# A recurrence and a dense block on one core: the first weights in 512 columns, own terms of two more units on TensorE, another written order

## The chip, the core and the metric

The kernel runs on one core of a Trainium2 chip. Five engines work side by side: TensorE (PE, with its weight loads shown apart as PEld), VectorE (DVE), ScalarE (ACT), GpSimd (POOL) and SyncE (SP). SP, ACT and POOL also issue transfers between HBM and the on-chip memory. The metric is the device time of one execution in microseconds, as a median over runs.

## The reference

Two blocks follow each other. The first is a recurrence with one state per head; its output, reshaped to 3072 rows of 384, goes through a dense block with 2048 hidden columns.

```python
# r, k, v: (4 batches, 8 heads, 768 steps, 48); w, u: (8, 48)
for t in range(S):
    kt, vt, rt = (k[:, :, t], v[:, :, t], r[:, :, t])
    cur = np.einsum('bhd,bhe->bhde', u[None] * kt, vt)
    y[:, :, t] = np.einsum('bhd,bhde->bhe', rt, state + cur)
    state = w[None, :, :, None] * state + np.einsum('bhd,bhe->bhde', kt, vt)
...
x = np.ascontiguousarray(attn_out.transpose(0, 2, 1, 3)).reshape(B * S, H * D)
h = x @ w_in          # (3072, 384) @ (384, 2048)
g = h - np.tanh(h)
return (g @ w_out).astype(np.float32)
```

The term with `u` is the *own term*: a step's own k and v, weighted by u. The weights `w_in` and `w_out` arrive as 64-bit floats, everything else as 32-bit.

## The kernel before, in words

**Units.** The recurrence is cut into 24 units, numbered 0 to 23: 64 steps of two batches with all heads, 12 chunks of time by two pairs of batches. A unit loads r, k and v (two halves of 96 KB each), turns r and k on TensorE, scales them by powers of the decay (`rT` and `kT`), and multiplies the two within the chunk (`levels`, rows `rT,kT` of L606). A predicated copy puts the part under the diagonal into the tile `at`. Then come the products with v (`outputs`, rows `at,vt`), with the state (`rT,state`) and for the next state (`vt,kw`). ACT copies the result into `xt`, the input of the dense block. Two units make one dense block of 256 rows; there are 12.

**Own terms.** Two ways exist. A unit with `n < OWN` makes `kU` from kT by four ACT operations (L709), multiplies it with rT on TensorE (rows `rT,kU`) and puts the diagonal into `at` by a predicated copy on DVE (L821). Any other unit multiplies r, k and u on DVE (`rk`, L696 and L824), sums over the head (`du`, L700) and writes the eight diagonals with eight ACT operations (L704). Before, `OWN` is 1, so unit zero alone goes the first way.

**The dense block.** A tile is 256 hidden columns of one block: six products for `h` (L217), five ACT and three DVE operations that make `g` from it, and four products for the output (`o`, L254; later a form with seven products, L307). The first pass goes over six blocks and the first four of the sixteen column groups of 128, and the units 0 to 11 run beside it.

**Weights.** They are loaded in 16 pieces of 128 x 768 numbers of 64 bits (768 KB): of each four, the first two are w_in (256 columns each), the others w_out. A w_in piece comes as four DMAs, two of 288 KB by SP and two of 96 KB by POOL, into one of four staging buffers; then DVE and ACT convert it to 32 bits in seven steps (L185 to L191, five on DVE).

**The order.** Nothing is scheduled while the program runs: the string `ORDER` names the tasks one after the other, two characters each, and each engine executes its own in that order. A task that waits holds up everything behind it on its engine. Names past the last task are *fills*, products of the identity with itself without use for the result (L534). The DMAs of SP and ACT together use eight landing marks in turn (`DMAHW0` to `DMAHW7` below), so that a ninth is issued only when the first has landed.

## Time and profile before

| | us |
|---|---|
| median of 3 runs | 582.31 (581.24 to 583.12) |
| the profiled execution | 582.57 |
| its span | 580.8 |
| PE busy | 562.5 (97%) |
| DVE busy | 429.9 (74%) |
| ACT busy | 404.3 (70%) |
| POOL busy | 199.9 (34%) |

The span goes from the first instruction to the last; the profiled execution's own time is 1.8 us longer. A share of busy time is a mean over stages: ACT's 70% is made of stages near 100% and stages near 55%. In groups of instructions each row has line, engine, operation, output and inputs, shapes and count, then busy time and mean ns, then the engine's idle time ahead of them and what ended it. In a timeline the row begins with start and length in us; neighbours on one engine are pipelined and overlap a little, so that the distance of two starts is the pace.

### The profile page before, as it was taken

What the parts mean: (1) busy time and instruction counts of PE and PEld (TensorE: products, weight loads), DVE (VectorE), ACT (ScalarE), POOL (GpSimd) and SP (SyncE); (2) the same over time, 40 slices, a digit from 0 to 9 for tenths busy, and PEclk for the clock granted to TensorE, in tenths of its full rate; (3) what the DMA queues carried; (4) which work ended last, traced back from release to release, by engine and by line L of the source; (5) the groups of instructions that cost most, each with busy time, mean ns of one, the idle gap of its engine ahead of it and who ended that gap; (6) DMA issues with size and microseconds to landing.
All of it is one profiled execution on the core that took longest, in us unless ns stands there. A gap on an engine that the chain in (4) does not pass through costs nothing.

```text
span 580.8 us, 14137 instructions
## 1 busy us (share of the span) xinstructions
PE 562.5 (97%) x5487; PEld 480.4 (83%) x5487; DVE 429.9 (74%) x720; ACT 404.3 (70%) x926; POOL 199.9 (34%) x366
## 2 busy tenths in 40 slices
PE   7699999999999999999999999999999999999995
PEld 4467777777776789999888889989999988999994
DVE  4899878999998787967699796567676766454534
ACT  2699999999977566545884787577577568765550
POOL 5201111300000233546256184273455253463430
PEclk9999999999999999999999999999999999999999
DMA  8987857594620000132344451441233000010001
GB/s 137 171 199 145 140 117 118 120 173 109 142 64 5 1 1 1 28 56 44 54 67 85 61 105 23 68 89 17 45 63 61 2 21 16 5 30 2 19 11 32
DMA packets 138549, 38.48 MB, mean 66 GB/s; under 512 B 130761, under 2 KB 132905, under 8 KB 138473
## 3 DMA queue, kind: packets, MB, share of 16 engines
q1 hardware_dynamic: 130140, 29.71, 28.7%
q0 software_dynamic: 4992, 6.99, 5.3%
q10 hardware_dynamic: 3340, 0.79, 0.9%
q8 instruction: 45, 0.74, 0.5%
q14 instruction: 32, 0.25, 0.2%
HBM read 31.66 MB, written 4.72 MB: 63 GB/s over the span
## 4 chain that ended last, share of the span: by engine, by line
PE 87%; DMA 4%; ACT 3%; DVE 2%; issue 1%; SPq 1%; POOL 0%; ACTq 0%; DVEq 0%; POOLq 0%
PE h L217 41%; PE p L307 26%; PE o L254 10%; PE yk_ps L606 6%; DMA rt<-in_r_dram 2%; PE x_ps L656 1%; DMA vt<-in_v_dram 1%; DMA xt<-rest 1%; ACT at L704 1%; PE x_ps L606 1%; SPq L644 1%; ACT xt L765 0%; PE p L254 0%; PE x_ps L534 0%; POOL xt L786 0%
## 5 line engine op out<-in xcount | busy, mean ns | idle before, releaser
L217 PE MATMUL h<-xt,w_in_sb 128*128 128x256 f32 x1152 | 267.3, 381 | 0.2 <-DMA xt<-rest 0.2
L217 PEld LDWEIGHTS h<-xt,w_in_sb 128*128 128x128 f32 x1152 | 214.9, 190 | 32.5 <-DVE g L242 1.5
L290 POOL TENSOR_TENSOR sg<-g 128x256 f32<-128x256 f32 x69 | 55.1, 800 | 197.7 <-DVE g L246 130.1
L242 DVE TENSOR_TENSOR g<-h,th 128x512 f32<-128x512 f32 x96 | 65.8, 686 | 67.9 <-ACT tg L233 25.2
L229 ACT ACTIVATE s<-h 128x512 f32<-128x512 f32 x96 | 57.1, 594 | 54.3 <-PE h L217 47.2
L307 PE MATMUL p<-mixed,sg 128*128 128x192 f32 x426 | 92.3, 327 | 0.0
L244 DVE TENSOR_TENSOR tg<-s,tg 128x512 f32<-128x512 f32 x96 | 69.3, 724 | 29.2 <-ACT s L224 19.4
L233 ACT ACTIVATE tg<-h 128x512 f32<-128x512 f32 x96 | 56.9, 594 | 41.9 <-PE h L217 29.9
L246 DVE COPY_PREDICATED g<-small,tg 128x512 f32<-128x512 int32 x96 | 72.0, 761 | 12.0 <-ACT small L235 9.0
L231 ACT ACTIVATE th<-h 128x512 f32<-128x512 f32 x96 | 56.7, 593 | 32.7 <-PE h L217 32.6
L307 PEld LDWEIGHTS p<-mixed,sg 128*128 128x128 f32 x426 | 73.3, 190 | 1.3 <-issue 0.3
L307 PE MATMUL p<-w_out_sb,g 128*128 128x192 f32 x284 | 70.4, 330 | 0.3 <-DVE o L335 0.3
L235 ACT ACTIVATE small<-s,smallb 128x512 f32<-128x512 f32 x96 | 68.5, 721 | 1.2
L254 PE MATMUL o<-w_out_sb,g 128*128 128x384 f32 x192 | 67.3, 489 | 0.0
L786 POOL DMA_DIRECT2D xt<-rest x66 | 32.5, 496 | 91.7 <-ACT rest L765 91.1
L224 ACT ACTIVATE s<-s 128x512 f32<-128x512 f32 x96 | 60.7, 633 | 1.4
L307 PEld LDWEIGHTS p<-w_out_sb,g 128*128 128x128 f32 x284 | 50.6, 190 | 3.1 <-DVE o L335 0.6
L254 PEld LDWEIGHTS o<-w_out_sb,g 128*128 128x128 f32 x192 | 35.8, 190 | 19.4 <-DVE parts L267 0.2
L704 ACT ACTIVATE at<-same,du 128x64 f32<-128x64 f32 x184 | 48.2, 342 | 0.5 <-DVE du L700 0.4
L292 POOL TENSOR_TENSOR sg<-sg,g 128x128 f32<-128x128 f32 x69 | 39.1, 569 | 3.1
L294 POOL TENSOR_TENSOR sg<-sg,g 128x128 f32<-128x128 f32 x69 | 37.2, 542 | 3.4
L307 PE MATMUL p<-mixed,g 128*128 128x192 f32 x142 | 34.7, 326 | 0.0
(127 smaller groups left out, 654.1 us busy)
## 6 DMA issues: line engine op xcount, KB each, us to landing
st<-in_moe_w_out_dram SPq DMA_DIRECT2D x8, 768.0 KB, 5.5
st<-in_moe_w_in_dram SPq DMA_DIRECT2D x16, 288.0 KB, 5.9
rt<-in_r_dram SPq DMA_DIRECT2D x46, 96.0 KB, 3.6
vt<-in_v_dram SPq DMA_DIRECT2D x46, 96.0 KB, 3.7
kt<-in_k_dram SPq DMA_DIRECT2D x44, 96.0 KB, 3.2
out_dram<-o POOLq DMA_DIRECT2D x44, 96.0 KB, 2.2
st<-in_moe_w_in_dram POOLq DMA_DIRECT2D x16, 96.0 KB, 5.9
parts<-in_k_dram SPq DMA_DIRECT2D x48, 32.0 KB, 2.1
```

The source lines that it names most:

```text
L217: self.nc.tensor.matmul(t.h2[:, z], self.w_in_sb[:, t.f // 2, kk, z * 128 : (z + 1) * 128], self.xts[t.j][:, kk].rearrange("p b t -> p (b ...
L224: A.activation(t.s, t.s, AF.Square, scale=G3)
L229: A.activation(out, t.h, AF.Arctan, scale=G2)
L231: A.activation(out, t.h, AF.Tanh)
L233: A.activation(out, t.h, AF.Tanh, scale=G1)
L235: A.activation(out, t.s, AF.Relu, bias=self.smallb, scale=-1.0)
L242: V.tensor_tensor(t.g, t.h, t.th, ALU.subtract)
L244: V.tensor_tensor(t.tg, t.s, t.tg, ALU.mult)
L246: V.copy_predicated(t.g, t.small.bitcast(I32), t.tg)
L254: self.nc.tensor.matmul(self.outs[i], t.g2[:, z, i * C : (i + 1) * C], self.w_out_sb[:, t.f + z, :], start=t.first and z == 0, stop=t.last ...
L290: add(t.s4[:, :2], g[:, 0::3], g[:, 1:2].to_broadcast([128, 2, C]), ALU.add)
L307: self.nc.tensor.matmul(ps[bank][:, half * n : (half + 1) * n], a, b, start=t.first and half == 0, stop=t.last, skip_group_check=True)
```

## The change

`OWN` becomes 3: units one and two take the way of unit zero. A pair of w_in pieces is loaded at once, 512 columns of a row in one run, into one staging buffer of double size (`si`, one of them), from which each half is converted by itself; w_out keeps its size with two buffers (`so`). Of the first pair all four DMAs are issued by SP, later ones two by SP and two by POOL as before. `ORDER` is another string from the first line to the last; its rows tell a reader nothing, so one of each is shown.

```diff
--- before.py
+++ after.py
@@ -32,7 +32,7 @@
 L = 2
 FIRST = 6
 PASSES = 4, 4, 8
-OWN = 1
+OWN = 3
 SWAP = 2
 ALONE = 2
 LATE = 4
@@ -43,50 +43,49 @@
 
 DIGITS = "0123456789ABCDEFGHIJKLMNOPQRSTUVWXYZabcdefghijklmnopqrstuvwxyz+_"
 ORDER = (
-    "00010J2f2g2h2i2j2k2l2m2n0HbWbX02030K040605bWbWbW2o2q3534363231332r2t0I2s07370A0FbWbX080B0C2u2x2y38392v092w3U0D3C"
...
+    "00012V2Q2P2R2T2S2U2W2X0H0KbCbD02030I040J0605bD2Y2a2r2q2s2o2b072c0AbD080B0C2e2n2p2h092f2i0D2g2Z2d2t2u2v0LbCbD2j0M"
...
 )
 
 
@@ -152,21 +151,34 @@
         if n % 4 > 1:
             f = slice(2 * of, 2 * of + 2)
             return self.w_out_sb[:, f, :], [(slice(0, 128), w_out.rearrange("(ko ki) f -> ki ko f", ki=128)[:, f, :])]
-        cols = w_in[:, of * 256 : (of + 1) * 256]
-        parts = []
+        return self.w_in_sb[:, of], self.spread(w_in[:, of * 256 : (of + 1) * 256])
+
+    def spread(self, cols):
+
+        d, parts = self.d, []
         for i in range(2):
             main = cols[: d.NK * 2 * d.D].rearrange("(k r) f -> r k f", k=d.NK)[i * d.D : (i + 1) * d.D]
             rest = cols[(2 * d.NK + i) * d.D :][: d.D].rearrange("(k x) f -> x k f", k=d.NK)
             parts += [(d.HEAD[i], main), (slice(i * PAD + d.D, (i + 1) * PAD), rest)]
-        return self.w_in_sb[:, of], parts
+        return parts
+
+    def wide(self, n):
+
+        return n % 4 < 2 and self.sources[0].dtype == I64
 
     def load(self, n, i, queue):
 
-        dst, parts = self.piece(n)
-        if self.sources[n % 4 > 1].dtype == I64:
+        if self.wide(n):
             if n not in self.staged:
-                self.staged[n] = self.stage.tile([128, self.COLS], I64, name="st", tag="st", bufs=4)
-            dst = self.staged[n].rearrange("p (k f) -> p k f", k=dst.shape[1])
+                self.staged[n] = self.staged[n + 1] = self.stage.tile([128, 2 * self.COLS], I64, name="si", tag="si", bufs=1)
+            dst = self.staged[n].rearrange("p (k f) -> p k f", k=self.d.NK)
+            parts = self.spread(self.sources[0][:, n // 4 * 512 : (n // 4 + 1) * 512])
+        else:
+            dst, parts = self.piece(n)
+            if self.sources[n % 4 > 1].dtype == I64:
+                if n not in self.staged:
+                    self.staged[n] = self.stage.tile([128, self.COLS], I64, name="so", tag="so", bufs=2)
+                dst = self.staged[n].rearrange("p (k f) -> p k f", k=dst.shape[1])
         to, src = parts[i]
         queue.dma_start(out=dst[to], in_=src)
 
@@ -175,12 +187,13 @@
 
 
         V, A = self.nc.vector, self.nc.scalar
-        dst = self.piece(n)[0].rearrange("p k f -> p (k f)")
-        st = self.staged.pop(n)
-        words = st.bitcast(U32).rearrange("p (n t) -> p n t", t=2)
-        lo, hi = words[:, :, 0], words[:, :, 1]
-        lo_f = st.bitcast(F32).rearrange("p (n t) -> p n t", t=2)[:, :, 0]
-        power = self.stage.tile([128, self.COLS], U32, name="power", tag="power", bufs=2)
+        dst, st = self.piece(n)[0], self.staged.pop(n).rearrange("p (k f) -> p k f", k=self.piece(n)[0].shape[1])
+        if self.wide(n):
+            st = st[:, :, n % 2 * 256 : (n % 2 + 1) * 256]
+        words = st.bitcast(U32).rearrange("p k (f t) -> p k f t", t=2)
+        lo, hi = words[..., 0], words[..., 1]
+        lo_f = st.bitcast(F32).rearrange("p k (f t) -> p k f t", t=2)[..., 0]
+        power = self.stage.tile([128, self.COLS], U32, name="power", tag="power", bufs=2).rearrange("p (k f) -> p k f", k=dst.shape[1])
         bits = dst.bitcast(U32)
         yield V.tensor_scalar(power, hi, 0x7FF00000, None, ALU.bitwise_and)
         yield V.tensor_scalar(bits, hi, 0xFFFFF, 0x100000, ALU.bitwise_and, ALU.bitwise_or)
@@ -586,9 +599,11 @@
         loads, converted = [], []
         for n in range(weights.count):
 
-            queues, data = (("SP",), (3.0,)) if n % 4 > 1 else (("SP", "POOL") * 2, (1.2, .95) * 2)
-            of = [add(e, .55, lambda n=n, i=i, e=e: weights.load(n, i, e_of[e]), [converted[n - 4] if n >= 4 else None],
-                      data=x, gated=True) for i, (e, x) in enumerate(zip(queues, data))]
+            wide, freed = weights.wide(n), [converted[n - 4]] if n >= 4 else []
+            queues, data = (("SP",), (3.0,)) if n % 4 > 1 else (("SP", "SP" if n < 2 else "POOL") * 2, (1.3, .98) * 2 if wide else (1.2, .95) * 2)
+            if not wide or n % 4 == 0:
+                of = [add(e, .55, lambda n=n, i=i, e=e: weights.load(n, i, e_of[e]), freed + ([converted[n - 3]] if wide and freed else []),
+                          data=x, gated=True) for i, (e, x) in enumerate(zip(queues, data))]
             if weights.sources[n % 4 > 1].dtype != I64:
                 converted.append(of[-1])
                 continue
```

What the string does is seen in each engine's own list. SP at the start, before (names: `st` staging, `rt`, `first_k`, `vt` the loads of unit zero, with numbers that are one higher for unit one):

```order
L171 DMA st<-in_moe_w_in_dram 48x3x256
L644 DMA rt_106<-in_r_dram 64x8x48
L644 DMA first_k_122<-in_k_dram 64x8x48
L644 DMA vt_116<-in_v_dram 64x8x48 [waits DMAHW0_49]
L171 DMA st<-in_moe_w_in_dram 48x3x256 [waits DMAHW1_49]
L644 DMA first_k_123<-in_k_dram 64x8x48 [waits DMAHW4_49]
L644 DMA rt_107<-in_r_dram 64x8x48 [waits DMAHW5_49]
```

and now:

```order
L659 DMA vt_116<-in_v_dram 64x8x48
L659 DMA rt_106<-in_r_dram 64x8x48
L659 DMA first_k_122<-in_k_dram 64x8x48
L183 DMA si<-in_moe_w_in_dram 48x3x512 [waits DMAHW0_49]
L183 DMA si<-in_moe_w_in_dram 16x3x512 [waits DMAHW3_49]
L183 DMA si<-in_moe_w_in_dram 16x3x512 [waits DMAHW4_49]
L183 DMA si<-in_moe_w_in_dram 48x3x512 [waits DMAHW6_49]
L659 DMA first_k_123<-in_k_dram 64x8x48 [waits DMAHW7_49]
L659 DMA rt_107<-in_r_dram 64x8x48 [waits DMAHW0_49]
```

Unit zero's loads moved ahead of all weights; the weights of two pieces stand as one group between unit zero and unit one, and what POOL issued of the first piece is in it.

DVE from unit zero's own-term copy into `at_132` on, before:

```order
L821 COPY_PREDICATED at_132<-same,x_ps_146 128x512
L807 TENSOR_TENSOR kw_113<-first_k_123,w_down 128x8x48
L807 TENSOR_TENSOR kw_112<-first_k_122,w_down 128x8x48
L696 TENSOR_TENSOR rk<-rt_107,first_k_123 128x384
L185 TENSOR_SCALAR power<-st 128x768
L186 TENSOR_SCALAR w_in_sb<-st 128x768
L660 TENSOR_TENSOR rT<-x_ps_150,power 128x512
L824 TENSOR_TENSOR rk<-rk,ub 128x384
L700 TENSOR_REDUCE du<-rk 128x8
L665 TENSOR_TENSOR kT<-x_ps_150,inverse 128x512
L189 SCALAR_TENSOR_TENSOR w_in_sb<-w_in_sb,st 128x768
L807 TENSOR_TENSOR kw_112<-kt,w_down 128x8x48
```

(L190 and the copy into `at_133`, L830, follow), and now:

```order
L836 COPY_PREDICATED at_132<-same,x_ps_146 128x512
L822 TENSOR_TENSOR kw_112<-first_k_122,w_down 128x8x48
L198 TENSOR_SCALAR power<-si 128x768
L199 TENSOR_SCALAR w_in_sb<-si 128x768
L198 TENSOR_SCALAR power<-si 128x768
L822 TENSOR_TENSOR kw_113<-first_k_123,w_down 128x8x48
L199 TENSOR_SCALAR w_in_sb<-si 128x768
L675 TENSOR_TENSOR rT<-x_ps_150,power 128x512
L680 TENSOR_TENSOR kT<-x_ps_150,inverse 128x512
L202 SCALAR_TENSOR_TENSOR w_in_sb<-w_in_sb,si 128x768
L845 COPY_PREDICATED at_133<-before,x_ps_150 128x512
L203 SCALAR_TENSOR_TENSOR power<-si,power 128x768
```

Behind these stand unit one's own-term copy (L836 into `at_133`) and then, ahead of unit two's copies, one `kw`, four long conversion steps (L204, L202, L203, L204), unit two's scaling of r, two short steps of the w_out piece and the flag. The first conversion steps of both halves moved ahead of unit one's scalings, and the three operations of its own terms (`rk`, `rk`, `du`) are gone.

ACT from unit one's `xt` (a row of 128x2x3x64) on, before:

```order
L765 COPY xt<-yk_ps 128x2x3x64
L795 ACTIVATE state_127<-yk_ps,power 128x2x48 x4
L704 ACTIVATE at_132<-same,du 128x64 x4
L572 ACT_TABLE_LOAD
L572 ACTIVATE warm<-one 128x1
L704 ACTIVATE at_132<-same,du 128x64 x4
L187 ACTIVATE power<-power,p_bias 128x768
L188 ACTIVATE st<-st 128x768
L229 ACTIVATE s<-h 128x512
```

and now:

```order
L780 COPY xt<-yk_ps 128x2x3x64
L707 COPY kT<-x_ps_146 128x512
L810 ACTIVATE state_127<-yk_ps,power 128x2x48 x4
L724 ACTIVATE kU<-kT,w_u 128x128 x4
L200 ACTIVATE power<-power,p_bias 128x768
L201 ACTIVATE so<-so 128x768
L246 ACTIVATE tg<-h 128x512
L242 ACT_TABLE_LOAD
L242 ACTIVATE s<-h 128x512
```

Unit two's own terms are four operations without the table load between them; the load moved behind the first `tg`.

More of the change, by code (lines that the diff above doesn't have):

```diff
@@ new lines @@
+    "3C0S2y2k2x3D3E0N2w0T3A2l2z0O2+393B2_0PbD33303F0Z342mbD310Q0U323I3X3J0V3b350R3a3c3K360W0F3M373L7v380X3Y3Z3N3G3H0a"
+    "3Q0E0b440Y0c3O45467w3R0d0s3P423h7z3g41430e3S7x3d7+3l0f3i3T853e3f3m3j4V3U863n4S3k4F3V3o4U4W4G3q0g4R4T3p0h4H7y483r"
+    "7_47494BbE3s4I814+804_504A3t3W4C824D3u834f4E3_3v89404b4y4K4J4g3+4x4z3x4h87843z4L883y3w4i5O0q0i4c8C4X8A4M4Y4Z4j8D"
+    "5M4a554N8J4d594O5L5N0j8K5P5Q4e4P8B0p5A4k4Q0k5B8E0l8V5s4l8M5r5t0m8L545u5C565v5w0n4m8N5Z8O8W0o4n528Q51538F58574o5a"
+    "8G6J5b8P4t4p6I6K8H4v8R5E4r6F8I8S5D4s6GbG6H4w4q8T5c4u5F5S635d5G5R5T645V8X0r5U655H5W8U6m5X5I5y5Y8j5J8Z5x5z8a6l6n5e"
@@ L90 @@
+    "ZfaCZ1Z3aEZ4Z2a0Z5Z6a1ZRZ7ZsZ8ZBZ9aHaQZDa3ZAaeZta4aSaFZSaGaIaRaJZgaTa5aUaVZha6aXa7aWafaKaYZCa+ahaLaiaMagZvalZuaj"
+    "a_Zwb0b3a8aZb2amb1a9akb4anaNaaabb5aOb6aoacb7apaqadaratauasavawb8axayazb9bAbB"
 )
```

78 lines of the change are left out of this document (35 added, 43 removed).

## The prediction

> **What bounds the kernel now.** I read the stage table first, in stretches of 10 us and, where data is short, of 5.
>
> ```profile
> 0.00:10.00 10.00, 7.96 (x23) 3.98 (x23) 4.71 (x13) 1.62 (x2) 5.76 (x26) 1.00 0.81 140
> 10.00:20.00 10.00, 7.76 (x198) 5.60 (x196) 7.35 (x14) 5.76 (x17) 3.97 (x12) 1.00 0.99 152
> 20.00:30.00 10.00, 5.52 (x142) 4.03 (x143) 6.97 (x12) 6.87 (x23) 1.01 (x2) 1.00 1.15 179
> 30.00:40.00 10.00, 10.00 (x243) 7.29 (x238) 9.28 (x17) 9.51 (x26) 0.00 (x0) 1.00 0.85 173
> 40.00:60.00 20.00, 19.17 (x347) 15.06 (x338) 19.82 (x35) 19.67 (x61) 3.92 (x8) 1.00 0.80 163
> ...
> 5.00:10.00 5.00, 4.49 (x18) 2.33 (x16) 3.55 (x5) 1.62 (x2) 1.48 (x3) 1.00 1.25 200
> 10.00:15.00 5.00, 3.84 (x88) 2.87 (x90) 2.38 (x5) 1.99 (x7) 2.01 (x8) 1.00 0.86 131
> ...
> 40.00:45.00 5.00, 4.48 (x103) 3.76 (x94) 5.00 (x9) 4.88 (x17) 2.31 (x5) 1.00 0.99 252
> ```
>
> The busy columns are PE, PEld, DVE, ACT, POOL; the last three are granted clock, DMA share and GB/s. PE stands idle 2.04 + 2.24 + 4.48 = 8.8 us before 30 us and hardly afterwards, so only the first stage has time to give. From 30 to 60 us DVE and ACT are nearly full as well. Some of the busy PE time yields nothing: products of the identity that fill waits (L534), here beside the one own-term product.
>
> ```profile
> L534 PE MATMUL h<-ident 128*128 128x512 f32 x12 | 7.1, 701 | 1.5 <-POOL ident masks.py:199 1.5
> L534 PE MATMUL h<-ident 128*128 128x256 f32 x8 | 2.9, 456 | 0.0
> L534 PE MATMUL x_ps<-ident 128*128 128x512 f32 x6 | 2.7, 592 | 0.0
> L534 PE MATMUL x_ps<-ident 128*128 128x256 f32 x4 | 1.3, 405 | 0.0
> L606 PE MATMUL x_ps<-rT,kU 48*64 48x64 f32 x32 | 1.0, 236 | 1.0 <-ACT kU L709 1.0
> ```
>
> These fills sum to 14.0 us. With the 8.8 idle, 22.8 of the first 40 us or so bring the result no nearer. Why PE waits there is in the chain of waits (start, length, what):
>
> ```profile
> 4.19 6.26 DMA vt<-in_v_dram
> ...
> 15.20 7.33 DMA rt<-in_r_dram
> ...
> 27.56 2.21 issue
> ```
>
> Loads set the first 23 us; the 2.21 us belong to ACT, which loads a table before it finishes unit two's own terms. The units' steps, from the timeline (the whole one to 24 us, PE's and single engines' behind it):
>
> ```profile
> 1.52 2.92 PE L534 MATMUL h<-ident 128*128 128x512 f32 x4 [1.52 <-POOL ident masks.py:199]
> 5.88 1.78 DVE L558 RECIPROCAL inverse<-power 128x260 f32<-128x260 f32 x1
> 8.37 1.28 ACT L560 ACT_TABLE_LOAD   x1 [8.37 <-DVE inverse L558]
> 8.84 1.46 PE L534 MATMUL h<-ident 128*128 128x512 f32 x4
> 9.04 0.69 DVE L660 TENSOR_TENSOR rT<-x_ps,power 128x512 f32<-128x512 f32 x1 [1.38 <-PE x_ps L656]
> 9.64 0.68 DVE L665 TENSOR_TENSOR kT<-x_ps,inverse 128x512 f32<-128x512 f32 x1
> 9.66 0.62 ACT L560 COPY twice<-inverse 128x512 f32<-128x512 f32 x1
> 12.23 0.97 ACT L709 ACTIVATE kU<-kT,w_u 128x128 f32<-128x128 f32 x3
> 12.63 0.97 PE L606 MATMUL x_ps<-rT,kU 48*64 48x64 f32 x32 [1.01 <-ACT kU L709]
> 13.66 0.75 DVE L821 COPY_PREDICATED at<-same,x_ps 128x512 f32<-128x512 int32 x1 [1.19 <-PE x_ps L606]
> 18.41 2.02 ACT L704 ACTIVATE at<-same,du 128x64 f32<-128x64 f32 x8 [0.38 <-DVE du L700]
> 22.66 0.63 PE L656 MATMUL x_ps<-ident,rt 128*128 128x128 f32 x4 [1.65 <-DMA rt<-in_r_dram]
> 23.22 0.58 PE L606 MATMUL yk_ps<-at,vt 64*64 64x64 f32 x24
> ...
> 32.32 0.69 PE L606 MATMUL yk_ps<-at,vt 64*64 64x64 f32 x32
> ...
> 46.26 0.69 PE L606 MATMUL yk_ps<-at,vt 64*64 64x64 f32 x32
> ...
> 47.83 2.75 PE L254 MATMUL o<-w_out_sb,g 128*128 128x384 f32 x8
> ...
> 32.28 0.95 DVE L189 SCALAR_TENSOR_TENSOR w_in_sb<-w_in_sb,st 128x768 f32<-128x768 uint32 x1
> 33.14 0.95 DVE L190 SCALAR_TENSOR_TENSOR power<-st,power 128x768 uint32<-128x768 uint32 x1
> ...
> 37.68 0.54 DVE L824 TENSOR_TENSOR rk<-rk,ub 128x384 f32<-128x384 f32 x1
> 38.15 0.72 DVE L830 COPY_PREDICATED at<-before,x_ps 128x512 f32<-128x512 int32 x1
> 38.78 0.53 DVE L700 TENSOR_REDUCE du<-rk 128x8 f32<-128x384 f32 x1
> ...
> 27.51 1.28 ACT L572 ACT_TABLE_LOAD   x1
> ```
>
> Outputs of units one, two and four start at 23.22, 32.32 and 46.26. Starts of neighbours give DVE's pace when nothing is waited for: 0.47 us for a short operation, 0.63 for a predicated copy, 0.60 for a scaling, 0.86 for a long conversion step.
>
> **The change, part by part.** Unit zero first. Its three loads now stand ahead of all weights on SP, so its k arrives no later, and ACT's DMA issues, which wait for earlier landings, should be through before the reciprocal ends at 7.66. Scaling and copying then start there, not at 9.04 and 9.66: kT is done by about 9.0, four kU (0.97 for three, so 1.3) by 10.4, the product (0.97) by 11.4, its predicated copy (0.75) by 12.1 instead of 14.4. That is 2.3 us; if k is as late as now, 0.9 of it remains (kT at 10.3).
>
> Own terms of units one and two. Removed for each: three short DVE operations (1.4 us) and eight ACT ones (2.02). Added: a predicated copy (0.63), 1.3 of kU, 0.97 on PE. That is 0.8 off DVE and 0.7 off ACT, and two products make 1.9 more on PE; where PE waits that costs nothing, where it doesn't, the 1.9. It is inside the path below.
>
> From unit zero's copy to outputs one, DVE's list now holds six short operations (2.8), two scalings (1.2), two long steps (1.7) and two predicated copies (1.3): 7.0. The second of these needs the first w_in load, all four DMAs of it, since both halves are converted here. So outputs one start at 12.1 + 7.0 = 19.1, or at the load's landing plus 6.5, whichever is later.
>
> The landing is the unknown, and no row shows a 512-column load. Until then six halves of unit zero (96 KB each), 1536 KB of weights and the two halves on ACT's queue must move, 2304 KB or 2.36 MB. The first 10 us carry 1.40 MB, of which 1.00 in the second five; so 0.40 by 5 us, and 1.96 MB remain. At 252 GB/s (the fastest row) they land at 12.8, at 200 at 14.8, at 131 (the slowest) at 20.0. I take 200, the row in which the same mixture moves now. Outputs one then start at 21.3 (19.3 to 26.5), where 23.22 stands; the r load that PE awaits at 22.66 is issued ahead of the w_out piece now and is due sooner.
>
> Outputs one to two. DVE's list is three short operations, four long, a scaling, the flag and two copies: 1.4 + 3.4 + 0.6 + 0.1 + 1.3 = 6.8; PE has four transposes (0.63) ahead of these outputs. So 7.4, against 9.1 now. (A conversion reads 256 of 512 staged columns, but as many elements as before; I cost it the same.) The table load, 1.28, moves behind outputs two. Outputs two to four take 13.9 now; with the table load inside I take 15.2. Outputs four: 21.3 + 7.4 + 15.2 = 43.9, that is 2.4 earlier than 46.26.
>
> By then the new order has also put a whole tile of output products through PE that the old one still has ahead of it (2.6 us, the row at 47.83), with equally many h tiles. From there ACT, at 19.67 of 20, sets the pace of the units in both, with equal work. At unit eleven the new order is half an h tile ahead, and level in output products: the 2.6 has become 1.3. So the gain is 2.4 + 1.3 = 3.7 us; ends 2.4 and 5.0 for this term alone, and 5.7 with the fast landing.
>
> Rest. Fills go from twenty-odd planned pieces to eight; priced by the rows above, 14.0 becomes about 8. That is the same gain seen from PE, not a second one: 6 less, 1.9 for own products back, near 4. Later w_in loads wait for both halves of the pair ahead (one buffer of double size); the first pass hides that, since its twelve tiles use the first pair alone. Issuing the first on SP alone frees POOL, which is idle anyway. After 60 us the written order differs everywhere, but PE was full; I take nothing, with 1.2 either way. The final products and output steps stand in the same order.
>
> The profiled execution took 582.57 (span 580.8 and 1.8 around it), 0.26 above the median of 582.31. 582.57 - 3.7 = 578.9, on the median **578.6**.
>
> [...]
>
> **The rivals.** *The late landing (slower).* All first weights go through one queue in a single load, and DVE, in order, stops at its first conversion; rT and kT of unit one, behind it, wait too. Price: landing plus 6.5. The gain of 3.7 at 14.8 is used up when it lands at 18.5; at 20.0, by the 131 GB/s row, it makes 1.5 us loss, 583.8. For it: DMA shares above 1 in the start. Against: 200 GB/s in the five microseconds that matter, and fewer, larger pieces. That these move no faster than the small ones, so that the change does nothing for its load, is in the 131 as well.
>
> *In-order slips (no change).* My steps are sums of one engine's list. If the 29.6 us of them stretch by a tenth because engines wait for each other in turn, 3.0 goes and 0.7 is left: 581.6. For it: ACT and DVE both near full.
>
> *Cold clock (no change or slower).* The first fills ran at 2.92 us where the same four records later took 1.46, so PE begins at half pace. With fewer fills, it might stay there or fall back; ten PE steps of about 0.6 on the path to outputs two, doubled in part, would cost some 4 us and leave 582.6. Against: 20 to 30 us, at 5.52 of 10 busy, keeps its pace. [...]
>
> **How the numbers follow.** The forecast 0.64, slips 0.19, late landing 0.11, cold clock 0.06. This kernel's runs lie within 0.3% of each other, 1.75 us, so faster means under 580.6. Forecast: nearly all of it faster; slips: a third faster, the rest same; cold clock: half same, half slower; late landing: slower. Faster 0.69, same 0.18, slower 0.13. The range runs from 575.5 (fast landing, 5.7, and 1.2 later) to 582.6 (cold clock, most of the slips); the forecast's own is 575.5 to 580.
>
> **What would show it.** Right: outputs one near 21, outputs four near 44, L534 in sum near 8 us, PE's idle before 30 us not above 9. Landing: idle DVE ahead of the first conversion. Slips: PE idle from 30 to 60 us above 2. Clock: products of 0.69 taking twice that after 10 us. It would be wrong in kind if the lead at 46 us were there and gone by 110, with new idle time of PE between.

## The result: slower by 2.8%

The changed kernel takes 599.17 us (median; 596.64 to 599.98) where the kernel before takes 581.77 on the same chip: a ratio of 1.0279, with a 95% interval of 1.025 to 1.0307. The forecast was 578.6, the range 575.5 to 582.6. The profiled execution took 598.64, its span is 596.9.

The stage table of the changed kernel (columns as in the prediction: PE, PEld, DVE, ACT, POOL busy, granted clock, DMA share, GB/s):

```profile
5.00:10.00 5.00, 3.45 (x50) 2.13 (x50) 3.88 (x5) 2.44 (x5) 2.04 (x8) 1.00 1.11 191
10.00:15.00 5.00, 4.09 (x98) 2.64 (x90) 1.89 (x3) 1.65 (x5) 0.27 (x1) 1.00 1.19 136
15.00:20.00 5.00, 0.00 (x0) 0.00 (x0) 0.00 (x0) 0.00 (x0) 0.00 (x0) 0.58 1.12 156
20.00:25.00 5.00, 3.28 (x41) 2.89 (x42) 3.82 (x5) 1.76 (x2) 0.27 (x1) 0.50 0.92 155
25.00:30.00 5.00, 4.42 (x70) 2.81 (x70) 3.96 (x7) 3.59 (x10) 0.00 (x0) 0.50 1.10 275
...
40.00:60.00 20.00, 14.26 (x334) 10.47 (x324) 19.04 (x37) 19.63 (x63) 3.81 (x7) 1.00 0.80 129
100.00:150.00 50.00, 47.55 (x488) 34.89 (x488) 45.36 (x71) 44.52 (x103) 6.82 (x14) 1.00 0.65 137
150.00:200.00 50.00, 47.64 (x183) 35.36 (x182) 44.22 (x67) 39.48 (x74) 1.02 (x2) 0.97 0.38 73
```

The kernel before, from 100 us on:

```profile
100.00:150.00 50.00, 50.00 (x315) 36.80 (x314) 46.97 (x74) 47.16 (x98) 6.94 (x14) 1.00 0.65 139
150.00:200.00 50.00, 50.00 (x195) 36.63 (x194) 46.12 (x72) 35.37 (x60) 2.33 (x3) 1.00 0.19 46
```

Three stretches have lost. From 15 to 20 us no engine works at all, while the DMA share is 1.12 at 156 GB/s, and the granted clock falls to 0.50 at about 15.8 us (0.58 is the mean of these five) and stands at 1.00 again from 33 us. From 40 to 60 PE works 14.26 of 20 (19.17 before). From 100 to 200 it works 95.2 of 100 (100.0 before). The steps behind these numbers, from the timeline (DVE first, then PE):

```profile
12.11 0.73 DVE L836 COPY_PREDICATED at<-same,x_ps 128x512 f32<-128x512 int32 x1
21.18 0.95 DVE L198 TENSOR_SCALAR power<-si 128x768 uint32<-128x768 uint32 x1 [7.90 <-DMA rt<-in_r_dram]
25.69 0.68 DVE L680 TENSOR_TENSOR kT<-x_ps,inverse 128x512 f32<-128x512 f32 x1
...
167.32 0.95 DVE L198 TENSOR_SCALAR power<-si 128x768 uint32<-128x768 uint32 x1 [2.46 <-DMA si<-in_moe_w_in_dram]
...
21.72 1.09 PE L671 MATMUL x_ps<-ident,first_k 128*128 128x128 f32 x4 [7.52 <-DMA first_k<-in_k_dram]
30.75 0.92 PE L621 MATMUL yk_ps<-at,vt 64*64 64x64 f32 x24
39.34 0.69 PE L621 MATMUL yk_ps<-at,vt 64*64 64x64 f32 x32
54.24 0.69 PE L621 MATMUL yk_ps<-at,vt 64*64 64x64 f32 x32
60.10 4.51 PE L230 MATMUL h<-xt,w_in_sb 128*128 128x256 f32 x12 [4.13 <-DMA xt<-rest]
```

Unit zero's own copy starts at 12.11 and is done at 12.84, near the forecast of 12.1. Then DVE stands 7.90 us ahead of its first conversion and PE 7.52 ahead of unit one's transposes. (The conversion's row names a load of r as what ended the wait; the step reads `si` alone, and the chain below names that.) Outputs one, two and four start at 30.75, 39.34 and 54.24, where 23.22, 32.32 and 46.26 stood. At 60.10 PE has waited 4.13 us for the transfers that fill tile one's x, and the twelve products behind that wait take 4.51 us, at a granted clock of 0.54 from 60 to 62 us, for 2.86 at 1.00 in the kernel before. The transfers and, for the kernel before, the transfers and the products:

```profile
50.48 2.92 POOL L801 DMA_DIRECT2D xt<-rest  x6 [13.57 <-ACT rest L780]
...
42.69 2.91 POOL L786 DMA_DIRECT2D xt<-rest  x6 [19.94 <-ACT rest L765]
52.89 2.86 PE L217 MATMUL h<-xt,w_in_sb 128*128 128x256 f32 x12
```

The chain of waits names what was late (start, length, what):

```profile
3.90 9.27 DMA vt<-in_v_dram
13.19 7.87 DMA si<-in_moe_w_in_dram
...
52.91 7.05 DMA xt<-rest
...
125.60 10.99 DMA si<-in_moe_w_in_dram
```

All of it is DMA: a half of unit zero's v that takes 9.27 us to land, on whose landing SyncE's last w_in issue waits (5.9 us, by the queue's own waits), that w_in DMA, landed at about 21.1, the transfers for x, and a later w_in pair.

### The profile page after: what moved, and what is told of

Same layout as the page of the kernel before. It is cut to its first block, busy times and chain, and to the rows that moved or that the text cites. A ratio compares the mean times of both kernels' runs of the same rounds, so it can differ in the third digit from the quotient of the medians.

```text
span 596.9 us, 14226 instructions
## 1 busy us (share of the span) xinstructions
PE 567.8 (95%) x5539; PEld 485.1 (81%) x5539; DVE 433.8 (73%) x716; ACT 403.8 (68%) x918; POOL 194.9 (33%) x356
## 4 chain that ended last, share of the span: by engine, by line
PE 76%; ACT 9%; DMA 8%; DVE 4%; issue 1%; POOL 1%; ACTq 0%; DVEq 0%; SPq 0%; POOLq 0%
PE h L230 36%; PE p L320 27%; PE yk_ps L621 6%; DMA si<-in_moe_w_in_dram 5%; PE o L267 5%; DMA vt<-in_v_dram 2%; ACT at L719 2%; ACT xt L780 1%; DMA xt<-rest 1%; ACT rest L780 1%; PE x_ps L671 1%; PE x_ps L621 1%; DVE power L198 1%; ACT power L200 1%; ACT small L248 1%
## 5 line engine op out<-in xcount | busy, mean ns | idle before, releaser
L230 PE MATMUL h<-xt,w_in_sb 128*128 128x256 f32 x1152 | 272.7, 385 | 8.8 <-DMA xt<-rest 4.5
L259 DVE COPY_PREDICATED g<-small,tg 128x512 f32<-128x512 int32 x96 | 73.6, 773 | 15.1 <-ACT small L248 12.5
L801 POOL DMA_DIRECT2D xt<-rest x66 | 32.5, 497 | 94.4 <-ACT rest L780 93.7
L719 ACT ACTIVATE at<-same,du 128x64 f32<-128x64 f32 x168 | 43.8, 341 | 1.8 <-PE yk_ps L621 1.0
```

The source lines that it names most:

```text
L230: self.nc.tensor.matmul(t.h2[:, z], self.w_in_sb[:, t.f // 2, kk, z * 128 : (z + 1) * 128], self.xts[t.j][:, kk].rearrange("p b t -> p (b ...
L259: V.copy_predicated(t.g, t.small.bitcast(I32), t.tg)
L719: A.mul(t.at[:, h % 2, h // 2], same, t.du[:, h : h + 1])
```

## The experiments

Theory A is that the 512-column load costs the time, theory B that the new order and the own terms lose it by themselves; the finer ones are named where they are put to the test. The kernel before is the common measure of all ratios. The edits are against the changed kernel unless something else is said.

Two things limit what small differences mean. The kernel before itself has medians from 581.5 to 583.0 us in the groups of runs, so two microseconds between kernels of different groups are not clear; the ratios take that out. And a position in the first stage is read from one execution. In four kernels with the same opening (the changed one, the two with fills and the one with another walk) unit zero's kT starts between 8.74 and 10.51 us and DVE's first conversion between 20.23 and 21.96.

### Narrow loads, the rest of the change kept

```diff
+            n, i = n + i // 2, i % 2
             if n not in self.staged:
-                self.staged[n] = self.staged[n + 1] = self.stage.tile([128, 2 * self.COLS], I64, name="si", tag="si", bufs=1)
+                self.staged[n] = self.stage.tile([128, self.COLS], I64, name="si", tag="si", bufs=2)
             dst = self.staged[n].rearrange("p (k f) -> p k f", k=self.d.NK)
-            parts = self.spread(self.sources[0][:, n // 4 * 512 : (n // 4 + 1) * 512])
+            parts = self.piece(n)[1]
+            to, src = parts[i + 2]
+            queue.dma_start(out=dst[to], in_=src)
...
-        if self.wide(n):
-            st = st[:, :, n % 2 * 256 : (n % 2 + 1) * 256]
...
-"SP" if n < 2 else "POOL"
+"POOL"
```

> The changed kernel with its own order and its three own-term products, but with every w_in pair loaded as before: two pieces of 256 columns, each in a tile of its own, the rests on POOL's queue. Theory A (the 512-column load is what costs): the first piece lands near 13 to 15 us, outputs one start at 20 to 22, PE is full from 100 us on as in the kernel before, the time is 576 to 583 us. Theory B (the written order and the own terms lose by themselves, whatever the load): outputs one still later than 28 us, time 595 to 600.

586.19 us, ratio 1.0075 (1.0049 to 1.01). So the load, with its queue, its buffer and the staging that the conversion reads, carries 13.0 of the 17.4 us, and the order still loses 4.4 with the old load. The two stages answer separately: the middle is cured, the transfers for x are not.

```profile
100.00:150.00 50.00, 50.00 (x435) 36.67 (x434) 47.37 (x75) 47.69 (x108) 9.89 (x20) 1.00 0.68 147
150.00:200.00 50.00, 50.00 (x199) 37.62 (x198) 46.07 (x74) 39.62 (x66) 0.00 (x0) 1.00 0.22 52
...
27.37 0.92 PE L622 MATMUL yk_ps<-at,vt 64*64 64x64 f32 x24
50.57 0.69 PE L622 MATMUL yk_ps<-at,vt 64*64 64x64 f32 x32
55.69 4.51 PE L231 MATMUL h<-xt,w_in_sb 128*128 128x256 f32 x12 [3.38 <-DMA xt<-rest]
```

Outputs one come at 27.37, 3.4 us ahead of the changed kernel but 4.2 behind the kernel before: theory A has the larger share, and neither has all of it: the 20 to 22 us for outputs one and the time of 576 to 583 were missed. Unit zero is later in this execution too (kT starts at 11.96 us, for 8.74; at 9.89 in a later kernel with the same opening).

### Short runs into the one buffer

```diff
-            dst = self.staged[n].rearrange("p (k f) -> p k f", k=self.d.NK)
-            parts = self.spread(self.sources[0][:, n // 4 * 512 : (n // 4 + 1) * 512])
+            for z in range(2):
+                dst = self.staged[n][:, z * self.COLS : (z + 1) * self.COLS].rearrange("p (k f) -> p k f", k=self.d.NK)
+                to, src = self.piece(n + z)[1][i]
+                queue.dma_start(out=dst[to], in_=src)
+            return
```

> The changed kernel, still the first pair by SyncE's queue alone and both halves into one tile at one point of the order, but each DMA of 512 columns issued as two of 256, so that a row's run is 2 KB and not 4 KB (eight DMAs a pair for four). Theory A1 (the length of the run is what costs): last landing of the first pair by 17 us at 190 GB/s or more, outputs one near 23, time 580 to 586. Theory A2 (the amount that must land before the first conversion costs, whatever its form): last landing near 21 as in the changed kernel, time 596 to 600. If the issues themselves cost (SyncE's queue waits per DMA), landing is later than 21 and the time above 600.

588.83 us, ratio 1.0115 (1.0091 to 1.0139): between the two theories. DVE's first conversion starts at 18.63, outputs one at 29.11. PE is full from 100 to 200 us again, although the loads are as coupled in the written order as before and the last pair, issued at 149.35, is read only at 160.88. A second difference had slipped in: the halves are read from contiguous staging here. It is taken apart below.

### The rests on two queues

```diff
-"SP" if n < 2 else "POOL"
+"POOL"
```

> The changed kernel with one word different: the rests of the first pair go by POOL's queue, as those of all later pairs do. Theory C (one queue alone is what makes the first load late): last landing near 16 to 17 us, outputs one near 25 to 26, time 591 to 594. Theories A and B: within 2 us of the changed kernel, 597 to 601, and the same late later pairs.

593.87 us, ratio 1.0216 (1.0183 to 1.0248). The last landing is at 18.37, outputs one at 27.60. Both are later than expected, the time is as expected: theory C holds, for 5.3 us by the medians and 3.7 by the ratios. In the changed kernel SyncE's four issues for the first pair take 9.3 us, 5.9 of them a wait for an older landing; here it has two to make. Whether the second queue does it, or the two issues fewer, was not separated.

### Unit one's inputs first

In SyncE's list:

```diff
+ first_k1<-in_k_dram, rt1<-in_r_dram, vt1<-in_v_dram
  si<-in_moe_w_in_dram (four)
- first_k1<-in_k_dram, rt1<-in_r_dram, vt1<-in_v_dram
```

> The changed kernel with the halves of unit one's k, r and v that stand behind the first w_in load moved ahead of it. Theory D (the first stage loses because unit one's inputs stand behind 1536 KB of weights, PE has nothing to do and its clock falls): unit one's k lands near 12 us, the granted clock stays above 0.9 until 20 us, time 592 to 595. Theory A: the four w_in DMAs are issued later by the moved 295 KB (1.5 to 2 us), DVE's first conversion starts at 22 to 23, time 598 to 602.

598.71 us, ratio 1.0283 (1.0249 to 1.0317). Unit one's transposes start at 14.35 for 21.72, and yet outputs one at 31.20: DVE still stands at its first conversion until 21.63, and the granted clock falls all the same, five microseconds later (1.00 from 15 to 20 us, 0.54 from 20 to 25). Theory D falls: what was late for PE was not the cause, since DVE's list is in order and the conversion stands ahead of unit one's scalings.

### Fills in the gap

In PE's list, ten fills, and in a later run five:

```diff
  yk_ps<-at0,vt0 and yk_ps<-at0,extra0 (outputs zero)
+ h<-ident 128x512 x10
  x1_ps0<-ident,first_k1 128x128 x4
```

> The changed kernel with ten more fills (products of the identity with 512 columns, about 0.72 us each) written into PE's list ahead of unit one's transposes, where PE stood idle for 8 us with the clock at half afterwards. Theory E (the late load costs a second time, because the clock falls to half until 32 us): the clock stays at 1.0 until 40 us, outputs four start 2 to 3 us sooner than 54.24, time 595 to 597. Rival (DVE sets the pace after the landing, so PE's pace is hidden): outputs four within 0.7 us of 54.24 and the time as that of the changed kernel, 598 to 600.

597.81 us, ratio 1.0249 (1.0198 to 1.03): it told nothing, since the ten fills ended at 26.6 us and stood in unit one's way.

> The changed kernel with five fills in PE's gap where an earlier run had ten, which then stood in unit one's way until 26.6 us. Five take about 3.6 us and should end before unit one's k lands. Theory E (the half clock from 15 to 32 us costs time): the clock stays above 0.9 until 25 us or more, the time from the last w_in landing to outputs one falls from 9.7 to 8.5 or less, time 596.5 to 598. Rival (DVE's list hides it): the interval stays at 9.4 or more, the time at 598 to 600.

595.76 us, ratio 1.0221 (1.0169 to 1.0272). The clock stayed up to 25 us, by the stage table of that kernel, and fell in part behind it:

```profile
15.00:20.00 5.00, 3.75 (x9) 1.33 (x7) 0.00 (x0) 0.00 (x0) 0.00 (x0) 1.00 1.14 151
20.00:25.00 5.00, 2.30 (x42) 1.71 (x42) 4.77 (x7) 1.77 (x2) 0.27 (x1) 1.00 0.88 170
25.00:30.00 5.00, 4.20 (x110) 3.31 (x114) 4.82 (x8) 3.82 (x10) 0.00 (x0) 0.75 1.10 249
```

Its last w_in landing is at 20.11 and its outputs one at 28.92, so 8.8 for 9.7, between the 8.5 of theory E and the 9.4 of its rival; it landed 0.9 sooner besides, which is within the spread of executions. So I estimate from the two intervals that the clock costs about 1 us by outputs one, perhaps more, as it was not up all the way (0.75 from 25 to 30 us). The 3.4 between the medians hold the sooner landing as well, and the intervals of the two ratios overlap.

### The transfers for x and the second pair

From here on the narrow kernel of 586.19 us is edited. First, the second pair's loads go behind the loads of the following units on SyncE's and GpSimd's queues:

```diff
- si<-in_moe_w_in_dram (two)
  rt2, kt, vt0, kt, rt0, vt1 (halves of later units)
+ si<-in_moe_w_in_dram (two)
  si<-in_moe_w_in_dram (two)
```

> The kernel with the narrow loads and the new order (586.2 us) with one thing moved: the second w_in pair's first loads stand later in SyncE's and GpSimd's lists, behind the loads of the units that follow, so that they are not in flight with the six transfers that fill tile one's x. Theory F (the 3.4 us that PE waits for these transfers, and the half clock after it, are a collision with the weights): the transfers land in 2 to 4 us for 5.2, PE's wait ahead of the twelve products is under 1 us, time 580 to 583. Rival (the new order asks for them too soon after they are issued, whatever else is in flight, or the rows of the units slow them): they still land in 4 us or more, PE still waits over 2 us, time 584.5 to 587.

584.39 us, ratio 1.0036 (1.0007 to 1.0064). Theory F holds for the wait and not for the time:

```profile
52.64 2.83 PE L231 MATMUL h<-xt,w_in_sb 128*128 128x256 f32 x12 [0.25 <-DMA xt<-rest]
71.07 0.67 PE L231 MATMUL h<-xt,w_in_sb 128*128 128x256 f32 x2 [0.30 <-DMA xt<-rest]
73.24 1.13 PE L231 MATMUL h<-xt,w_in_sb 128*128 128x256 f32 x4 [1.50 <-DMA xt<-rest]
```

Tile one's wait is gone, and its products take 2.83 us again. But the pair, now issued as a lump at 62.5, runs beside the transfers for tile two: they wait 1.8 us in turn. The collision moved.

Then unit one's inputs go ahead of the first weights as above, and in DVE's list:

```diff
  kw0
+ kw1, rT, kT (unit one)
  power<-si, w_in_sb<-si (both pieces)
- kw1, rT, kT (unit one)
```

> The kernel of the run before this one (narrow loads, second pair later) with two things more: unit one's k, r and v ahead of the first weights on SyncE's queue, and the first steps of the conversion behind unit one's scalings in DVE's list. If the first stage's loss is that units wait behind weights (theory D with the narrow load): unit one's k lands near 12 us for 20.1, outputs one start at 22 to 24 for 27.4, time 2 to 4 us below the run before it, 577 to 580. If DVE's work until outputs two sets the pace anyway: within 1.5 us of it.

584.60 us, ratio 1.0046 (1.0014 to 1.0077), no gain over the run before. Outputs one came at 25.38, one to two took 9.9 us, and outputs four started at 50.47 for 50.65. The wait only moved: DVE now stands 2.30 us for the second piece behind unit one's scalings (until 20.32), ahead of its predicated copies, and PE behind it works at a granted clock of 0.54 from 20 to 25 us and 0.78 from 25 to 30.

### Loads alone

A kernel of its own that only loads, stage by stage.

> Loads alone; it leaves out the whole computation and writes zeros. Stages, each begun when the one before has landed: a wide w_in pair (four DMAs of 512 columns, 1536 KB); two narrow pieces (eight DMAs of 256 columns, the same bytes); one narrow piece; one and two w_out pieces; one main DMA of 512 and of 256 columns, and two at once; a wide pair with the rests on POOL; six halves of a unit alone on ACT's queue; the wide pair, the narrow pieces and two w_out pieces each with those six halves. Theory A1 (4-KB runs are slower by themselves): the wide pair takes 1.3 times the narrow pieces' time or more, alone too. Theory G (4-KB runs only hurt what shares the engines with them): alone the two take the same, 6 to 8 us; with the six halves the wide pair's halves land 1.5 times later than the narrow one's. If neither: all within a tenth, and the 21 us are the waits of the queue ahead of the issue.

DVE reads each load when it has landed. The first DMAs of the stages below were issued at 1.34 (`aww`), 15.12 (`am`), 39.27 (`aq`), 92.61 (`bww`) and 111.77 (`bn`); the reads, from DVE's timeline:

```profile
14.78 0.17 DVE L130 COPY seen<-aww 128x3 uint32<-128x3 uint32 x1 [13.47 <-DMA aww<-in_moe_w_in_dram]
22.26 0.17 DVE L130 COPY seen<-am 128x3 uint32<-128x3 uint32 x1 [7.15 <-DMA am<-in_moe_w_in_dram]
26.93 0.17 DVE L130 COPY seen<-am 128x3 uint32<-128x3 uint32 x1 [4.50 <-DMA am<-in_moe_w_in_dram]
...
45.59 0.17 DVE L130 COPY seen<-aq 128x3 uint32<-128x3 uint32 x1 [1.75 <-DMA aq<-in_moe_w_out_dram]
...
110.84 0.17 DVE L130 COPY seen<-bww 128x3 uint32<-128x3 uint32 x1 [18.23 <-DMA bww<-in_moe_w_in_dram]
122.82 0.17 DVE L130 COPY seen<-bn 128x3 uint32<-128x3 uint32 x1 [11.04 <-DMA bn<-in_v_dram]
128.01 0.17 DVE L130 COPY seen<-bn 128x3 uint32<-128x3 uint32 x1 [5.02 <-DMA bn<-in_moe_w_in_dram]
```

The wide pair (`aww`) takes 13.4 us with nothing else in flight. The narrow pieces (`am`) take 11.8, and the first of them is there after 7.1. The same bytes of w_out (`aq`) take 6.3. With six halves of a unit beside them the wide pair takes 18.2, the narrow pieces 11.0 and 16.2. So run length is worth an eighth (1.14, under the 1.3 of A1), the halves beside a wide pair land in 8.6 to 9.8 us (medians) for 6.7 to 7.3 beside a narrow one and 3.0 to 3.2 alone, and neither theory sees the main thing: w_in loads take twice as long as w_out loads, in either width. From 3 to 14 us the wide pair moves 135 GB/s at a DMA share of 0.89, from 41 to 45 w_out moves 373 at 0.94. A wide pair with its rests on GpSimd's queue takes 13.0 us, so a second queue by itself gains 0.4.

Then single loads in other shapes.

> Single loads, each begun when the one before has landed and been read; the computation is left out and zeros are written. w_in columns into 128 partitions (three rows a partition) in runs of 2 and of 4 KB; w_in half rows of 8 KB into 128 partitions; w_out rows of 3 KB into 48 partitions and into 128; the kernel's own main DMA (48 partitions) in both widths. Theory P (few partitions make the w_in loads slow): into 128 partitions the 2- and 4-KB runs move at 250 GB/s or more, w_out into 48 partitions at 180 or less. Theory S (pieces of long rows, 16 KB apart in DRAM, are slow to read): 128 partitions change nothing, 150 to 185, and w_out into 48 partitions keeps 250 or more.

The issues stand at 7.50 (`mww`), 22.27 (`ofw`), 28.45 (`oa`) and 33.10 (`wfw`); DVE's reads:

```profile
16.44 0.17 DVE L124 COPY seen<-mww 128x4 uint32<-128x4 uint32 x1 [8.97 <-DMA mww<-in_moe_w_in_dram]
28.12 0.16 DVE L124 COPY seen<-ofw 48x4 uint32<-48x4 uint32 x1 [5.88 <-DMA ofw<-in_moe_w_out_dram]
32.74 0.17 DVE L124 COPY seen<-oa 128x4 uint32<-128x4 uint32 x1 [4.30 <-DMA oa<-in_moe_w_out_dram]
39.08 0.16 DVE L124 COPY seen<-wfw 48x4 uint32<-48x4 uint32 x1 [6.01 <-DMA wfw<-in_moe_w_in_dram]
```

It is the partitions. 576 KB of w_out into 48 partitions (`ofw`) take 5.9 us, as long as the kernel's own main DMA of that size (`wfw`, 6.0) and longer than 768 KB into 128 (`oa`, 4.3). 1536 KB of w_in in the same 4-KB runs land in 8.9 us when they go into 128 partitions (`mww`), for 13.4 in the kernel's four DMAs of 48 and 16 partitions, and `mww` was not even alone: twelve stores of zeros (192 KB each), issued by ACT from 1.29 us on, were still in flight. The DMA engines moved, in all:

```profile
8.00:16.00 8.00, 0.00 (x0) 0.00 (x0) 1.00 1.01 374
```

So 8.9 is an upper bound for that load. Its own rate is 176 GB/s, short of the 250 that theory P named, and the 2-KB runs into 128 partitions (5.8 us for 768 KB) ran beside the same kind of stores. Theory P holds by `ofw` and `oa`, and theory S falls: w_out into 48 partitions moves 100 GB/s, not 250. Two main DMAs of 576 KB at partitions 0 and 64 take 9.8 us, one takes 6.0. Why few partitions take longer was not shown, and a load into 16 alone was not run.

### Half of the load at a time

```diff
+            if n < 4:
+                z, i = divmod(i, 2)
+                dst = self.staged[n][:, z * self.COLS : (z + 1) * self.COLS].rearrange("p (k f) -> p k f", k=self.d.NK)
+                for to, src in self.piece(n + z)[1][i::2]:
+                    queue.dma_start(out=dst[to], in_=src)
+                return
             dst = self.staged[n].rearrange("p (k f) -> p k f", k=self.d.NK)
```

The second kernel has `n >= 4` instead. The first of them has the first pair's rests on GpSimd's queue too.

> The changed kernel with only the first w_in pair loaded as two pieces of 256 columns (rests on POOL's queue); the three later pairs stay wide. Half of the load's cost should be seen apart: outputs four near 50.6 as with all pairs narrow (54.24 changed), the late landings from 100 to 200 us stay (PE 95 to 96 of 100 busy there), time 593 to 596. If the later pairs cost nothing (all 13.0 us that the narrow loads give back come from the start): 585 to 588.

591.15 us, ratio 1.013 (1.008 to 1.0181), a little under what was expected: outputs four at 51.14, and PE at 95.5 of 100 from 100 to 200 us, as in the changed kernel.

> The other half: the first pair as in the changed kernel (512 columns, SyncE's queue alone), the three later pairs as pieces of 256 columns into the two halves of the one buffer, both still issued only when the pair ahead is converted. Outputs four near 54; if the length of a run is what makes the later pairs late: PE full from 100 to 200 us, time 589 to 592. If the single buffer for both halves is what does: PE 95 to 96 of 100 there, time 593 to 598.

588.47 us, ratio 1.0111 (1.0066 to 1.0157): outputs four at 53.49, and PE full from 100 to 200 us. Alone, the first pair's half of the edit takes 8.0 us off and the later pairs' half 10.7; both together took 13.0 (by the ratios 8.7, 9.8 and 11.9). The two do not add; that each spares PE some of the same waits is likely and not shown. The first half's 8.0 has the second queue in it, worth 5.3 alone. Against the all-narrow kernel the first pair wide costs 2.3 us by the medians and the later pairs wide 5.0, but by the ratios 2.1 and 3.2, with intervals that overlap; what is clear is PE's 95.5 of 100 with the later pairs wide. The single buffer for both halves is not what costs, since it stayed.

### The conversion's walk

The later pairs' trouble had two candidates left: the loads, and the conversion. Its first two steps, by line, in the changed kernel:

```profile
L198 DVE TENSOR_SCALAR power<-si x8: 939/949/958, 21.2 to 189.4; 128x768 uint32<-128x768 uint32 x8
L198 DVE TENSOR_SCALAR power<-so x8: 541/554/562, 35.4 to 200.0; 128x768 uint32<-128x768 uint32 x8
```

The same step on as many elements takes 949 ns from the wide staging (`si`, three rows of 256 out of 512) and 554 from w_out's contiguous one (minimum, median, maximum). The edit changes only the order in which the elements are walked:

```diff
+        by_two = [x.rearrange("p k (z f) -> p z k f", z=2) for x in (power, hi, bits)] if self.wide(n) else [power, hi, bits]
-        yield V.tensor_scalar(power, hi, 0x7FF00000, None, ALU.bitwise_and)
-        yield V.tensor_scalar(bits, hi, 0xFFFFF, 0x100000, ALU.bitwise_and, ALU.bitwise_or)
+        yield V.tensor_scalar(by_two[0], by_two[1], 0x7FF00000, None, ALU.bitwise_and)
+        yield V.tensor_scalar(by_two[2], by_two[1], 0xFFFFF, 0x100000, ALU.bitwise_and, ALU.bitwise_or)
```

> The changed kernel with the first two DVE steps of a w_in conversion walking their elements in another order: two times three rows of 128 instead of three rows of 256; the same elements, staging and loads. In the changed kernel these steps take 0.949 and 0.942 us from the wide staging and 0.554 from a narrow one. [...] Rival (the stride of the wide staging is what costs): the steps stay at 0.94, time 598 to 600.

```profile
L199 DVE TENSOR_SCALAR power<-si x8: 545/558/567, 21.1 to 183.8; 128x768 uint32<-128x768 uint32 x8
...
100.00:150.00 50.00, 48.66 (x461) 36.20 (x452) 45.43 (x73) 45.74 (x106) 6.83 (x14) 1.00 0.61 124
150.00:200.00 50.00, 48.25 (x191) 35.75 (x189) 45.20 (x71) 39.99 (x69) 1.02 (x2) 1.00 0.40 75
```

593.98 us, ratio 1.0186 (1.0129 to 1.0243): 5.2 us less by the medians, the edge of the 594 to 597.5 that were forecast, with every load as it was. Outputs one start at 29.89, 0.9 sooner (1 to 1.6 forecast). The step takes 558 ns for 949 (0.55 to 0.6 us forecast), next to the 554 of the contiguous staging, with the stride of the wide staging as it was: the rival falls, and it is the order of the walk. What in three rows of 256 makes it slow was not shown. From 100 to 200 us PE now works 96.9 of 100, for 95.2: the walk was 1.7 us of the loss there, and by subtraction 3.1 are left to the loads.

### A version that beats both

Narrow loads and the new order, with the lump taken apart. SyncE's list:

```diff
  vt0, rt0, first_k0
+ first_k1, rt1, vt1
  si (two, the first piece)
- si (two, the second piece)
- first_k1, rt1, vt1
  kt x2, rt2 x2
+ si (two, the second piece)
  vt2
  ...
- si (two, the second pair's first piece)
  rt2 x2
+ si (two, the second pair's first piece)
  kt x2
+ si (two, the second pair's second piece)
```

A piece's conversion waits for that piece alone, and the first one stands behind unit one's first predicated copy in DVE's list.

> A kernel that should beat both if theory H holds (a w_in pair holds all DMA engines for about 12 us, narrow or wide, and whatever is in flight with it is late; so the lump costs, not the order): narrow loads, the new order with unit one's inputs ahead of the first weights, the second piece of the first pair behind unit two's k and r, conversions behind unit one's predicated copies, and the second pair's two pieces on SyncE's queue between the transfers for tile one and tile two. Theory H: outputs one at 20 to 22 us, outputs four at 45 to 47, no wait for x over 0.5 us until 80 us, time 576 to 580. If ACT and DVE set the pace of the first 50 us whatever lands when: outputs four at 49 to 51, time 581 to 584.

580.37 us against 582.97, ratio 0.9958 (0.9938 to 0.9977): faster than both, by 0.4% against the kernel before.

```profile
20.34 0.58 PE L622 MATMUL yk_ps<-at,vt 64*64 64x64 f32 x24 [0.30 <-issue]
33.69 0.69 PE L622 MATMUL yk_ps<-at,vt 64*64 64x64 f32 x32
48.87 0.69 PE L622 MATMUL yk_ps<-at,vt 64*64 64x64 f32 x32
51.42 2.83 PE L231 MATMUL h<-xt,w_in_sb 128*128 128x256 f32 x12 [0.81 <-DMA xt<-rest]
...
24.54 1.11 PE L672 MATMUL x_ps<-ident,kw 128*128 128x128 f32 x4 [3.26 <-DVE kw L823]
```

Outputs one stand where the forecast for the change had them (20.34 for 21.3), and the wait for x is 0.81 (up to 0.5 expected). Outputs four come later than expected: after outputs one PE waits 3.26 us for `kw`, which in DVE's list stands behind four conversion steps and a wait of 0.47 for the second piece, and the granted clock is 0.67 from 20 to 30 us. So theory H is borne out by the first stage. Its 45 to 47 for outputs four was missed, and 580.37 lies between its 576 to 580 and the rival's 581 to 584.

## Why the prediction was wrong

**Unit zero** was nearly right: kT done at 9.4 and the own copy at 12.84, the forecast 9.0 and 12.1. The gain was lost in the 7.9 us for which DVE then stood ahead of the first conversion.

**The landing of the first w_in load** is the step that failed first. It was priced at 14.8, by the 200 GB/s of one row of the stage table, with bounds of 12.8 and 20.0; it measured about 21.1, outside them. The row was of another mixture. In the changed kernel 191 GB/s held from 5 to 10 us, then 136 and 156, nearer to the 131 and 174 of the rows that stood behind the chosen one. From these rows I estimate that the priced 2.36 MB had moved by about 18 us; by 21.1 some 2.8 MB had, as loads issued behind the weights moved beside them. The last w_in DMA was not even issued before 13.2 us, since SyncE waited 5.9 us for a landing mark, a wait that the sum does not have. The rate is the larger part of it all the same: with unit one's inputs first, all four were issued by 10.4 us, behind three more halves, and the last landed at 21.6. The right price could be had from loads alone: the four DMAs take 13.4 us with nothing beside them, 18.2 with six halves beside them. The rival of the late landing had the mechanism, the place and the sign, but 0.11 of the chance, and its own price (landing plus 6.5) gives 584.9 for 21.1. The landing thus explains 6.3 of the 20.6 us between forecast and result; the rest is in the steps that follow. Unit one's k on SyncE's queue was there no sooner than the weights ahead of it (landed at about 21.1, the transposes behind it at 21.72, and at 14.35 where unit one's inputs stood first); but time came from moving it only where the conversion let DVE go on.

**"Landing plus 6.5"** measured 9.7. The 6.5 summed DVE's list alone. The two wide conversion steps of each piece took 0.94 instead of the 0.55 of a contiguous one (four of them, 1.6 us), and the chain from kT to outputs one runs through PE twice, at a granted clock of 0.50 (25 to 30 us): kT at 25.69, outputs one at 30.75.

**The table of the units** held otherwise: outputs one to two took 8.6 (7.4 forecast), two to four 14.9 (15.2). Outputs four at 54.24 for 43.9 is the landing (6.3), the list behind it (3.2) and 0.9 of steps. With the wait for x and the slow products behind it (4.1 and 1.7) and PE's idleness from 100 to 200 us (4.8) that makes 21.0, for 20.6; it is read from one execution, so the closeness is in part luck.

**"A conversion reads 256 of 512 staged columns, but as many elements as before; I cost it the same"** was wrong by 0.39 us a step, 6.3 us of DVE over sixteen steps. Walking them in another order gave back 5.2 us.

**"Later w_in loads wait for both halves of the pair ahead; the first pass hides that"** was wrong: PE loses 4.8 us from 100 to 200, most of it at two conversions for which DVE waited 2.0 and 2.5 us. With narrow pieces in the same buffer it loses nothing. Of the 4.8, the walk of the conversion is 1.7; the other 3.1 stay, by subtraction, with the wide loads, whose pairs, issued at 125 and 154 us, land after 11.0 and 12.7.

**"ACT, at 19.67 of 20, sets the pace of the units in both"** missed the transfers for x. The order issues them at 50.5 and wants them at about 56; in the kernel before they were issued at 42.7 and used at 52.9. The 4.1 us of waiting and the slow products behind it are a price of the new order, and stay with narrow loads (3.4); with the second w_in pair moved from beside them the wait is 0.25, but comes back at tile two. The 1.3 us that the order was to gain here could not be seen.

**Fills** were priced at about 8 and are 10.2 (5.9 + 3.2 + 1.1 by line); 1.0 of the difference is the clock, two pairs of 1.22 us at 0.50 where 0.70 stands in the kernel with five fills. **In-order slips** showed their sign, PE idle 6.2 us from 30 to 60 for the 2 named, but 4.1 of it is the wait for x. **Cold clock** came, as a consequence of the landing: the granted clock is 0.50 from about 15.8 us on, 1.6 into the gap. By the estimate above it costs about 1 us by outputs one; the 3.4 between the medians hold more than the clock.

**The gain of 3.7** was not measured by itself. With the load's lump taken apart, an edited order and the own-term products give 2.6 us by the medians; how much of that is the own terms was not tried. The range's lower end is 575.4 by its own terms, not 575.5.

## What to carry to other kernels

Price a load by its own shape, above all by the partitions it writes (576 KB into 48 took 5.9 us, 768 KB into 128 took 4.3), and not by the mean rate of the stage in which it will stand; then ask which in-order engine stands still until all of it has landed (here DVE, for 7.9 us). A load made larger can cost twice over: in what shares the engines with it (halves of a unit landed in 8.6 to 9.8 us beside the wide pair, in 6.7 to 7.3 beside the narrow pieces), and in the steps that read it in another walk (949 ns for 554). If the first stage is bound by transfers, spread the weights between the inputs, in pieces that each release some work.

## What the runs showed of the hardware

- 1536 KB of w_in: 13.4 us as DMAs into 48 and 16 partitions, 8.9 or less into 128 (beside stores). 576 KB into 48 partitions: 5.9 (w_out, 3-KB rows) and 6.0 (w_in, 4-KB runs). Two of 576 KB at partitions 0 and 64: 9.8. Runs of 2 KB instead of 4 made 11.8 of the 13.4.
- Halves of a unit in 192-byte rows land in 3.0 to 3.2 us alone, and in 8.6 to 9.8 beside a wide w_in pair.
- A DVE step on 768 elements: 949 ns walked as 3 rows of 256, 558 as 2 by 3 rows of 128.
- In the changed kernel the granted clock fell from 1.00 to 0.50 at about 15.8 us, 1.6 after PE's last product, and after 7.5 us without work it stayed at 0.50 until 32.5 us and stood at 1.00 from 33, although PE was busy 3.28 of 5 from 20 us and 4.42 of 5 from 25; with five fills in the gap it stood at 1.00 until 25 us.
